# Emptying the filter's PSUM banks on two engines, splitting the last quad, and moving two casts to GpSimd

## The chip, the cores and the metric

The kernel runs on one core of a Trainium2 chip. The metric is the device time of one execution in microseconds. Where a few tenths of a microsecond matter, the text also gives the length of one stage in the profiled execution, because the stage can be read to 0.1 us while whole executions spread by more.

## The reference

The reference filters eight sequences of 3008 steps and 256 channels in the frequency domain, and passes every step through a feed-forward layer with a squared ReLU:

```python
def _attn_ref(x, filt_r, filt_i):            # x: (8, 3008, 256)
    X = np.fft.rfft(x, axis=1)
    F = (filt_r + 1j * filt_i)[None, :, :]
    return np.fft.irfft(X * F, n=x.shape[1], axis=1).astype(np.float32)

def _moe_ref(x, w_in, w_out):                # x: (24064, 256), w_in: 256 x 2048
    h = np.maximum(x @ w_in, 0.0)
    return (h * h @ w_out).astype(np.float32)
```

The kernel does the transforms as matrix products (stages A and B forward, P and Y back). After the first sequence has been filtered, the feed-forward products begin, and they fill the rest of the time. The change touches only the first sequence, ahead of the feed-forward products.

## The kernel before

PSUM is given out from rings: `psF` and `psO` are single banks (two each), and `psH` are double banks (two). A bank means here 128 x 512 in F32, as the program's tiles have it. The filter is spread over the partitions by matmuls (`psf`, im = 0 for its real part, im = 1 for its imaginary part), scaled and emptied to `sF` in SBUF:

```python
    def place_f(im, k, *engs, rotate=False):
        ...
            t = psH(f"psf_{im}_{k}")
            banks, groups = [t[:, 0, :], t[:, 1, :]], [(t, 0)]
        ...                                   # matmuls with sPF into the two banks
        for t, i in groups:
            eng = engs[i % len(engs)]
            ...                               # eng empties t into sF
```

VectorE multiplies stage B's result by the filter (`prods`). Stage P takes two of these products, four blocks of steps together (a quad), into a double bank; ScalarE empties it to `ze`, and `ze` is written to memory, to be read back in another layout (`zt`) by stage Y:

```python
    def unit_p0(k):
        ...
        ps = psH(f"psP_0_{k}")
        for i in range(4):                    # products with sSP and sSPx into ps
            ...
        nc.scalar.copy(out=ze, in_=ps.rearrange("p t (a d) -> p (t a) d", d=D))
        nc.sync.dma_start(out=dZ[0]..., in_=ze)
```

The units are called in this order, with `unit_b` standing for stage B and its product:

```python
    for k in range(2):
        cast_wide(1, k, nc.gpsimd, nc.gpsimd)
    for k in range(7):
        if k < 6:
            unit_b(0, 2 * k)
            if k < 5:
                place_f(1, k + 1, nc.scalar)
            unit_b(0, 2 * k + 1)
        if k > 0:
            unit_p0(k - 1)
        if k < 4:
            place_f(0, k + 2, nc.scalar)
    cast_wide(1, 2, nc.vector, nc.scalar)
    ...                                       # reads of z, loads of w_out, stage A of the next sequence
    for n in range(4):
        unit_y(0, n)
```

## Time and profile before

| what | before |
|---|---|
| time, median of 3 runs (lowest to highest) | 794.04 us (793.07 to 794.68) |
| first product of VectorE in this stage starts | 24.42 us |
| last product ends | 40.39 us |
| last emptying of `ze` ends | 42.08 us |
| first real matmul of stage Y (`psY` from `zt`) | 48.26 us |
| first feed-forward matmul (`psH`) | 49.71 us |

Times in profile lines count from the start of the profiled execution. In a list in order of time, a line gives the start, the busy time, the engine (PE is TensorE, DVE VectorE, ACT ScalarE, POOL GpSimd), the line of the program, the operation, output and input, and how many instructions the line gathers; a bracket gives the idle time of the engine before it and what ended it ("listed idle" below is the sum of these; some waits under 0.2 us are not listed). "Stage" below means the time from the start of VectorE's first product to the end of the last emptying of `ze`: 42.08 - 24.42 = 17.66 us here.

### The profile page before, as it was taken

Reading aid. Unit: us, or ns where it says so; the run is one execution under the profiler, and the core shown is the slowest. Engines: PE = TensorE matmul, PEld = TensorE weight load, DVE = VectorE, ACT = ScalarE, POOL = GpSimd, SP = SyncE. Lnnn points to the kernel's source line nnn. Section 1 sums busy time; section 2 is a strip of 40 time slices with the busy share of each in tenths; the row PEclk is TensorE's granted clock in tenths of the full one; section 3 lists DMA queues with packets and bytes.
Section 4 is the critical chain, followed back from the end, with each engine's and each line's share of the span. In section 5 each row is a group of like instructions: output and inputs, shape, how many; then the busy total and the mean of one; then the engine's idle time right before and its main releaser. Section 6 shows DMA issues by size and latency. Waiting matters only on the chain.

```text
span 791.9 us, 14822 instructions
## 1 busy us (share of the span) xinstructions
PE 778.9 (98%) x6102; PEld 552.5 (70%) x6102; DVE 550.3 (69%) x897; ACT 557.4 (70%) x711; POOL 23.6 (3%) x36
## 2 busy tenths in 40 slices
PE   8989999999999999999999999999999999999998
PEld 5746667667676777867777676776767677676666
DVE  6866994579755897559965699556995579553342
ACT  3976776777777777767776777676777777776664
POOL 3800000000000000000000000000000000000000
PEclk9999999999999999999999999999999999999999
DMA  9994554346814557154562555424563332611111
GB/s 363 368 260 153 146 157 111 93 135 167 205 42 112 167 155 180 48 173 135 132 167 65 163 147 155 112 80 148 159 180 86 97 133 66 147 40 41 41 41 54
DMA packets 88571, 107.32 MB, mean 136 GB/s; under 512 B 6336, under 2 KB 79040, under 8 KB 84288
## 3 DMA queue, kind: packets, MB, share of 16 engines
q1 hardware_dynamic: 88296, 106.19, 46.5%
q8 instruction: 48, 0.79, 0.4%
q10 hardware_dynamic: 144, 0.18, 0.1%
q14 instruction: 19, 0.16, 0.1%
q0 software_dynamic: 64, 0.00, 0.0%
HBM read 58.12 MB, written 48.23 MB: 134 GB/s over the span
## 4 chain that ended last, share of the span: by engine, by line
PE 89%; DVE 6%; DMA 3%; ACT 1%; SPq 0%; issue 0%; DVEq 0%; ACTq 0%
PE psO L579 40%; PE psH L562 38%; PE psA L361 3%; PE psY L532 2%; PE psB L445 2%; DMA f<-in_filt_i_dram 2%; PE psP L496 2%; DVE prod L453 2%; DVE h L570 1%; DMA wout<-in_moe_w_out_dram 1%; PE psf L287 1%; PE psf L290 1%; DVE yf L467 0%; ACT sF L298 0%; DVE yf L461 0%; ACT h L566 0%
## 5 line engine op out<-in xcount | busy, mean ns | idle before, releaser
L566 ACT ACTIVATE h<-psH 128x1024 f16<-128x1024 f32 x376 | 384.9, 1024 | 189.3 <-PE psH L562 186.7
L579 PE MATMUL psO<-sWout,h 128*128 128x256 f16 x3008 | 388.9, 272 | 0.6 <-DVE h L570 0.6
L562 PE MATMUL psH<-yt,sWin 128*128 128x512 f16 (+7 forms) x1728 | 386.9, 351 | 1.6 <-DVE yt L541 0.7
L579 PEld LDWEIGHTS <-h 128*128 128x128 f16 x3008 | 290.6, 98 | 79.1 <-DVE h L570 0.9
L570 DVE TENSOR_TENSOR h<-h 128x1024 f16<-128x1024 f16 x376 | 252.6, 685 | 104.7 <-ACT h L566 104.5
L562 PEld LDWEIGHTS <-sWin 128*128 128x128 f16 x1728 | 159.5, 98 | 101.7 <-issue 3.3
L453 DVE TENSOR_TENSOR prod<-psB,sF 128x1024 f16<-128x1024 f32 x84 | 102.3, 1218 | 2.8 <-PE psB L445 2.8
L541 DVE CAST yt<-psY 128x376 f16<-128x376 f32 x62 | 34.0, 549 | 59.4 <-PE psY L532 59.4
L367 DVE CAST u<-psA 96x512 f16<-96x512 f32 x50 | 34.3, 687 | 47.3 <-PE psA L361 45.1
L498 ACT CAST ze<-psP 128x512 f16<-128x512 f32 x84 | 49.1, 585 | 17.2 <-PE psP L496 14.7
L590 ACT COPY ost<-psO 128x512 f32<-128x512 f32 (+1 forms) x96 | 55.8, 581 | 6.8 <-PE psO L579 5.3
L532 PE MATMUL psY<-sC,zt 112*128 112x94 f16 x512 | 42.4, 205 | 1.4 <-DMA zt<-dZ 1.4
L532 PEld LDWEIGHTS <-zt 112*128 112x128 f16 x512 | 35.1, 98 | 11.6 <-issue 1.6
L467 DVE TENSOR_TENSOR yf<-prod,yf 128x512 f16<-128x512 f16 x84 | 35.7, 425 | 2.9
L361 PE MATMUL psA<-x,sC 94*96 94x512 f16 x96 | 36.6, 382 | 0.0
L445 PE MATMUL psB<-ut,sSB 128*128 128x256 f16 x192 | 36.5, 273 | 0.0
L496 PE MATMUL psP<-yf,sSP 128*128 128x256 f16 x168 | 32.1, 272 | 0.5 <-DVE prod L453 0.3
L539 ACT CAST yt<-psY 128x376 f16<-128x376 f32 x66 | 30.9, 468 | 2.0 <-issue 1.7
L445 PEld LDWEIGHTS <-sSB 128*128 128x128 f16 x192 | 18.5, 98 | 19.5
L340 DVE CAST x<-x 94x2048 f16<-94x2048 f32 x24 | 29.2, 1216 | 0.0
L365 ACT CAST u<-psA 96x512 f16<-96x512 f32 x50 | 28.6, 572 | 0.0
L460 DVE COPY yf<-prod 64x512 f16<-64x512 f16 x84 | 24.3, 289 | 2.9
(65 smaller groups left out, 253.2 us busy)
## 6 DMA issues: line engine op xcount, KB each, us to landing
x<-in_x_dram SPq DMA_DIRECT2D x20, 768.0 KB
zt<-dZ SPq DMA_DIRECT2D x64, 192.0 KB
dU<-u SPq DMA_DIRECT2D x28, 384.0 KB
dZ<-ze SPq DMA_DIRECT2D x28, 384.0 KB
out_dram<-ost SPq DMA_DIRECT2D x66, 128.0 KB
out_dram<-ost SPq DMA_DIRECT2D x31, 256.0 KB
ut<-dU SPq DMA_DIRECT2D x7, 1024.0 KB
xw<-in_x_dram SPq DMA_DIRECT2D x6, 1024.0 KB
```

Source lines behind the costliest of these rows:

```text
L361: nc.tensor.matmul(ps[0:96, :], sSA, x16s[(b, c)][:, m, :], start=True, stop=True)
L445: nc.tensor.matmul(ps[:, i * D:(i + 1) * D], sSB[:, 2 * p + i, :], uts[b][:, 2 * p + i, :], start=True, stop=True)
L453: nc.vector.tensor_mul(out=prod, in0=ps.rearrange("p (a d) -> p a d", d=D).unsqueeze(1).to_broadcast([128, 2, 2, D]), in1=sF[:, :, 2 * p:2 ...
L467: nc.vector.tensor_add(out=yf, in0=prod[:, 0], in1=yf)
L496: nc.tensor.matmul(ps[:, i * D:(i + 1) * D], sSP[:, 2 * p + i, :], yf[:, i, :], start=True, stop=True)
L498: nc.scalar.copy(out=zes[(b, c)][:, 2 * i6:2 * i6 + 2, :], in_=ps.rearrange("p (a d) -> p a d", d=D))
L532: nc.tensor.matmul(ps[:, 94 * jj:94 * jj + 94], zt[:, 4 * (g % 2) + jj, dt * 128:(dt + 1) * 128], sSY, start=True, stop=True)
L562: nc.tensor.matmul(ps[:, i, o:o + n], sWin[:, dt, jt * 128:(jt + 1) * 128], yts[b][:, dt, r:r + n], start=(dt == 0), stop=(dt == 1))
L566: nc.scalar.activation(out=h2[:, 2 * s:2 * s + 2, :], in_=ps, func=AF.Relu)
L570: nc.vector.tensor_mul(out=v, in0=v, in1=v)
L579: nc.tensor.matmul(pso[g][:, t % 2, :], h2s[g][:, jt, t * 128:(t + 1) * 128], sWout[:, jt, :], start=(jt == 0), stop=(jt == NJT - 1))
L590: nc.scalar.copy(out=ost[:, h0:h0 + step, :], in_=pso[g][:, h0:h0 + step, :])
```

## The change

Its intent is to relieve ScalarE, which empties three double banks in every round of 3.3 us. Part 1 gives half of each emptying of the filter's real part to VectorE (four times). Part 2 puts the last quad of stage P into two single banks and empties it in three pieces, so that its second half alone comes after the last product. Part 3 moves two casts of the next input from VectorE and ScalarE to GpSimd.

```diff
-    def place_f(im, k, *engs, rotate=False):
+    def place_f(im, k, *engs, rotate=False, halves=False):
...
-            banks, groups = [t[:, 0, :], t[:, 1, :]], [(t, 0)]
+            banks = [t[:, 0, :], t[:, 1, :]]
+            groups = [(t[:, i:i + 1, :], i) for i in range(2)] if halves else [(t, 0)]
...
-        ps = psH(f"psP_0_{k}")
+        if k == 5:
+            ps = [psF("psP_0_5a"), psF("psP_0_5b")]
+        else:
+            t = psH(f"psP_0_{k}")
+            ps = [t[:, 0, :], t[:, 1, :]]
...
-        nc.scalar.copy(out=ze, in_=ps.rearrange("p t (a d) -> p (t a) d", d=D))
+        if k < 5:
+            nc.scalar.copy(out=ze, in_=t.rearrange("p t (a d) -> p (t a) d", d=D))
+        else:
+            nc.scalar.copy(out=ze[:, 0:2, :], in_=ps[0].rearrange("p (a d) -> p a d", d=D))
+            nc.scalar.copy(out=ze[:, 2, :], in_=ps[1][:, 0:D])
+            nc.vector.tensor_copy(out=ze[:, 3, :], in_=ps[1][:, D:2 * D])
...
-    for k in range(2):
+    for k in range(3):
         cast_wide(1, k, nc.gpsimd, nc.gpsimd)
...
-            place_f(0, k + 2, nc.scalar)
-    cast_wide(1, 2, nc.vector, nc.scalar)
+            place_f(0, k + 2, nc.scalar, nc.vector, halves=True)
```

More of the change, by code (lines that the diff above doesn't have):

```diff
@@ L481, in unit_p0 @@
             for v, w in enumerate((sSP[:, c2, :], sSPx[c2 // 12][:, c2 % 12, :])):
-                nc.tensor.matmul(ps[:, i // 2, (i % 2) * D:(i % 2) * D + D], w,
+                nc.tensor.matmul(ps[i // 2][:, (i % 2) * D:(i % 2) * D + D], w,
                                  prod[:, v, i % 2, :], start=(v == 0), stop=(v == 1))
-        nc.scalar.copy(out=ze, in_=ps.rearrange("p t (a d) -> p (t a) d", d=D))
+        if k < 5:
[4 more added lines that the diff above has]
+            nc.vector.tensor_copy(out=ze[:, 3, :], in_=ps[1][:, D:2 * D])
         nc.sync.dma_start(
```

## The prediction

> **What bounds the kernel now.** I read the page first (busy shares), then the chain of waits between 24 and 61 us, then the order of time on ScalarE, VectorE and TensorE between 20 and 50 us. The page says that TensorE is busy 98% of the span, so nearly everything is a feed-forward stage that the change does not touch. The change acts between 24 and 47 us. What counts is therefore when the feed-forward stage starts, about 50 us in, because after that start the program is the same. The chain of waits gives the way there (start us, us, what):
>
> ```profile
> 29.93 1.12 ACT sF L298
> ...
> 33.25 1.12 ACT sF L298
> ...
> 38.04 2.36 DVE prods L453 x2
> 40.44 0.61 PE psP L482 x4
> 41.07 1.02 ACT ze L484
> 42.11 2.38 DMA dZ<-ze
> 44.63 0.31 SPq L514
> 45.05 5.91 DMA wout<-in_moe_w_out_dram
> 50.96 1.03 ACT h L566
> ```
>
> Up to 38 us the chain runs through ScalarE emptying the placement of the filter (sF); then it goes over to VectorE's last two products, the last quad of stage P, its eviction ze, the write of dZ, and the reads and loads that are queued behind that write. So whatever delays the last ze delays all that follows. In order of time (start us, us busy, engine, line, what, idle before), ScalarE has one round like this, and VectorE the whole stage like this:
>
> ```profile
> 31.02 1.01 ACT L484 CAST ze<-psP 128x1024 f16<-128x1024 f32 x1
> 32.16 1.02 ACT L298 ACTIVATE sF<-psf 128x1024 f16<-128x1024 f32 x1
> 33.25 1.11 ACT L298 ACTIVATE sF<-psf,sign 128x1024 f16<-128x1024 f32 x1
> 34.34 1.01 ACT L484 CAST ze<-psP 128x1024 f16<-128x1024 f32 x1
> ```
>
> ```profile
> 24.42 7.06 DVE L453 TENSOR_TENSOR prods<-psB,sF 128x1024 f16<-128x1024 f32 x6
> 32.44 2.35 DVE L453 TENSOR_TENSOR prods<-psB,sF 128x1024 f16<-128x1024 f32 x2 [0.96 <-ACT ze L484]
> 35.77 4.62 DVE L453 TENSOR_TENSOR prods<-psB,sF 128x1024 f16<-128x1024 f32 x4 [0.98 <-ACT ze L484]
> 40.30 0.68 DVE L222 CAST xw<-xw 128x1024 f16<-128x1024 f32 x1
> ```
>
> A round of ScalarE is 34.34 - 31.02 = 3.32 us for three evictions of 1.01 to 1.11 us: it is full. But VectorE, too, is nearly full: from 24.42 to 40.39 us (35.77 + 4.62) it has twelve products and idles only twice, 0.96 + 0.98 = 1.94 us in all. That 1.94 us is all the room it has for new work.
>
> [...] on ScalarE 1024 columns take 1.012 us and 512 take 0.598, on VectorE 1.22 and 0.68, so halves cost more than half. [...] VectorE's cast of 128x1024 f takes 1.51 us at 20.56 while GpSimd casts too, against 0.68 to 0.69 alone.
>
> **Part 1: halves of the placement.** Four evictions of psf on ScalarE (1.02 us each, the four with im = 0, k = 2 to 5) become a ScalarE half (0.598 in the group of 512 columns) and a VectorE half (0.68; back to back about 0.60, from three casts of ut that take 2.40 us with one of 1.22). ScalarE is relieved of about 4 x 0.45 = 1.8 us. VectorE gets 4 x 0.60 = 2.4 us, more than its 1.94 us of room. Even if every idle moment vanished, its last product would end at 40.39 + 2.4 - 1.94 = 40.85.
>
> It won't go that well, as the built program shows in its semaphore waits:
> - Each VectorE half waits for a count of ScalarE that is exactly that of the other half of the same tile, not for TensorE. The halves lie in two banks, yet they run one after the other: I count this as a fact of the program, whatever made it so.
> - VectorE's queue is product 0, 1, half 2, product 2, 3, half 3, 4, 5, half 4, 6, 7, half 5, 8 to 11. A half that waits for ScalarE holds up the products behind it.
> - The ring of the two double banks has changed places once: psP_0 now waits for the eviction of psf_1_2 instead of psf_0_2, and psf_0_3 for the VectorE half of psf_0_2.
>
> I step through it with these durations: eight matmuls of a bank pair 0.87 us (0.109 apart), 0.2 us from the last one's start plus its drain to the eviction, product 1.165 (7.06 for six in a row, less the overhang), 0.05 us for a wait that is met. The same stepping for the kernel before ends ze at 42.03; the trace has 42.08, so the method may be trusted to about 0.1 us.
> - Products 0 and 1 end at 26.75, half 2 at 27.36, products 2 and 3 at 29.69.
> - psf_1_2 is emptied from 26.56 to 27.67 as before; psP_0 starts at 27.72 instead of 26.61, fills to 28.59, psf_0_3 to 29.47. ScalarE empties ze 0 from 28.79 to 29.80, then its half of psf_0_3 to 30.37. VectorE, free since 29.69, does half 3 from 30.42 to 31.03: 0.7 us idle.
> - Products 4 and 5 end at 33.36; ScalarE's half of psf_0_4 ends at 33.74; half 4 runs from 33.79 to 34.40. Products 6 and 7 end at 36.73; half 5 runs from 37.16 to 37.77. Idle 0.43 twice.
> - Products 8 to 11 follow without a gap: 37.77 + 4 x 1.165 = 42.43.
>
> Against 40.39 that is **+2.0 us** for the last product (work +2.4, idle 0.7 + 0.43 + 0.43 = 1.56 in place of 1.94).
>
> **Part 2: the last quad.** Before: from the end of the last product, 40.39, to the end of ze, 42.08, 1.69 us. After: 0.05 wait, four matmuls 0.44, drain 0.2, ScalarE's last 256 columns (an estimate by the two sizes above: 0.39), wait 0.04, VectorE's 256 columns (likewise 0.41), one after the other [...]: 1.53 us. The first half of the quad has long been emptied. **Gain 0.16 us.**
>
> **Part 3: casts of x on GpSimd.** VectorE loses 0.68 us at 40.30 and ScalarE 1.05 us at 41.98; GpSimd, which is done at 39.14, gets two more of about 1.0 us (3.99 for four) and ends near 41.2. The chunk that needs them is the third, whose matmuls run from 44.4 us on. And the 24 matmuls of stage A run 0.218 us apart without one gap, so ScalarE's cast held up nothing: TensorE next waited for the read of z:
>
> ```profile
> 46.56 0.27 PE L530 MATMUL psY<-zero 128*128 128x128 f16 x2 [0.29 <-ACT u L390]
> 48.26 0.33 PE L532 MATMUL psY<-sC,zt 112*128 112x94 f16 x4 [1.42 <-DMA zt<-dZ]
> ```
>
> Gain: none. In the changed kernel stage A would start at 42.93 and end near 48.2, and z land at 48.26 + 1.9 = 50.2, still later.
>
> **Sum.** +2.04 - 0.16 + 0 = +1.9 us on the last ze; the write of dZ, both loads of w_out and the reads of z stand behind it in one queue in the same order, so the feed-forward stage starts 1.9 us later. 794.04 + 1.9 = **795.9 us**.
>
> **Rivals.**
> - What the change was made for: ScalarE was full and on the chain, so relieving it by 0.45 us in four rounds shortens the stage. For it: the three evictions of ScalarE fill 3.14 of 3.32 us. Against: TensorE works through 28 matmuls of 0.109 us in a round, 3.05 us, so a round can gain 0.27 us at most, about 1.1 us in four; and VectorE can't give that, as the sum without waits (40.85) shows. If both halves ran side by side, my stepping puts ze at about 42.5 to 42.9: +0.4 to +0.8, a time near 794.6. If I am wrong about VectorE altogether and the tail and the freed casts count: 793.
> - The delay is absorbed, as the transfers behind are the bound anyway: the DMA engines are full from 47 to 60 us. Against: they are idle from 42 to 43 us just because they wait for ze, and the loads are issued after the reads of z. If half were absorbed: 795.
> - VectorE is held up further: GpSimd's two added casts run beside products 9 to 11. The products that ran beside GpSimd took 1.168 us each, those half beside it 1.133; at most 0.1 us. Worse would be waits of the ring that I have mis-stepped: one eviction more in the chain is 1.1 us, 797.
>
> **Range and chances.** The runs of before spread 793.07 to 794.68, about 0.8 us either way, and my stepping may be off by 0.5 us: 794.7 to 797.0. Two per cent are 16 us; the whole stage that is changed lasts 17, and nothing else moves. Within 2%: 0.98; either side 0.01.
>
> **What would show it right or wrong.** Right: in the changed profile VectorE's 512-column casts of psf start just after ScalarE's halves end and are waited for as "ACT sF"; VectorE's idle time before its halves is about 1.5 us and before its products near nothing; its last product ends near 42.4; the chain of waits runs through VectorE in the whole stage; psY's first real matmuls start near 50.2 and the first eviction h near 52.9; the idle time of TensorE before psP grows. The third part is right if stage A's matmuls remain 0.218 us apart. The prediction is wrong if the halves overlap in time, if the last ze ends before 42.1, or if psY starts within 0.5 us of 48.26 although ze is late.

The order, which the 1.53 us of Part 2 count as 0.39 + 0.04 + 0.41, is in the trace of the changed kernel: ScalarE's quarter runs from 43.27 us for 0.37 us, VectorE's from 43.67 us for 0.42 us, and VectorE's idle time before it is ended by "ACT ze". The 0.2 us called drain can be read in the trace of the kernel before: the last matmul of the last quad starts at 40.77 us, one interval of 0.109 us later it is 40.88, and `ze` starts at 41.07.

## More of the kernel before

One view sums the busy time of each engine over the 17.7 us of the stage. Its columns are the window, its length, and then TensorE, weight loads, VectorE, ScalarE and GpSimd with their instruction counts, the granted TensorE clock, the DMA engines' share and GB/s:

```profile
24.40:42.10 17.70, 16.49 (x152) 13.69 (x150) 14.70 (x14) 15.62 (x16) 14.23 (x21) 1.00 0.89 335
```

TensorE, VectorE, ScalarE and GpSimd are each busy 80% of this window or more, the weight loads 77%.

## The result, and the profile after

The changed kernel took 795.49 us in the median of six runs (795.30 to 797.36); the kernel before 793.42 us in the median of its six (793.07 to 794.68). The ratio is 1.003, with a 95% interval of 1.0017 to 1.0043: within 2%, and slower by some 2 us. Here and below a ratio is the mean time of one kernel's fast runs over the mean of the other's in the same rounds, so it is not quite the ratio of the quoted medians. All kernels gave correct results.

| us | before | after | predicted |
|---|---|---|---|
| first product starts | 24.42 | 24.55 | 24.42 |
| last product ends | 40.39 | 42.58 | 42.43 |
| idle of VectorE between its products | 1.94 | 1.70 | 1.56 |
| last product to last `ze` | 1.69 | 1.51 | 1.53 |
| first real matmul of stage Y | 48.26 | 50.32 | 50.2 |
| stage | 17.66 | 19.54 | |

VectorE of the changed kernel, in order of time:

```profile
24.55 2.36 DVE L454 TENSOR_TENSOR prods<-psB,sF 128x1024 f16<-128x1024 f32 x2
26.82 0.68 DVE L303 CAST sF<-psf 128x512 f16<-128x512 f32 x1
27.42 2.35 DVE L454 TENSOR_TENSOR prods<-psB,sF 128x1024 f16<-128x1024 f32 x2
30.55 0.69 DVE L303 CAST sF<-psf 128x512 f16<-128x512 f32 x1 [0.78 <-ACT sF L299]
...
37.37 0.69 DVE L303 CAST sF<-psf 128x512 f16<-128x512 f32 x1 [0.41 <-ACT sF L299]
37.97 4.61 DVE L454 TENSOR_TENSOR prods<-psB,sF 128x1024 f16<-128x1024 f32 x4
43.67 0.42 DVE L494 CAST ze<-psP_5b 128x256 f16<-128x256 f32 x1 [1.09 <-ACT ze L493]
```

The halves are the casts of 128x512. From the second on they wait for "ACT sF", ScalarE's half of the same double bank, and the idle time that the kernel before had ahead of its products now stands ahead of them. The third half (34.01 us, 0.51 us of idle) is in the cut. The chain of waits (start, length, what) shows a round of the changed kernel, and then the end of the stage:

```profile
33.38 0.61 ACT sF L299
33.98 0.02 issue
34.01 0.70 DVE sF L303
34.71 0.04 issue
34.75 1.03 PE psP L487 x8
...
40.23 2.36 DVE prods L454 x2
...
43.27 0.38 ACT ze L493
43.65 0.02 issue
43.67 0.44 DVE ze L494
44.11 0.01 issue
44.12 2.38 DMA dZ<-ze
```

Before, one emptying of 1.12 us stood in this chain. Now ScalarE's half, VectorE's half and a handover stand there one after the other (33.38 to 34.71 us, 1.33 us), and TensorE's next product with SPt waits for them. The sums of the same 17.7 us show what the relief of ScalarE was worth:

```profile
24.40:42.10 17.70, 15.70 (x143) 12.69 (x141) 15.99 (x17) 12.88 (x15) 16.32 (x23) 1.00 0.85 320
```

ScalarE went from 15.62 to 12.88 us. The relief in this is 4 x (1.02 - 0.60) = 1.68 us; most of the rest is one emptying of `ze` (1.01 us) that the changed kernel has not reached at 42.1 us. TensorE, too, did less in the same time (15.70 for 16.49 us). Over its own, longer stage (24.55 to 44.10 us) ScalarE is busy for 13.70 us: its freed time became idle time.

One more thing in the profiled execution must be set apart, as it is not part of the change. It took 797.24 us, 1.8 us more than four other runs of the changed kernel (795.30 to 795.56). Its first feed-forward matmuls are slower, and the windows show why (the clock is the third number from the end):

```profile
50.32 0.33 PE L542 MATMUL psY<-sC,zt 112*128 112x94 f16 x4 [1.30 <-DMA zt<-dZ]
...
51.78 4.49 PE L572 MATMUL psH<-yt,sWin 128*128 128x512 f16 x12 [0.28 <-ACT yt L549]
```

```profile
51.60:55.00 3.40, 3.08 (x7) 0.96 (x7) 0.85 (x2) 1.15 (x2) 0.00 (x0) 0.50 1.06 245
55.00:56.00 1.00, 1.00 (x6) 0.50 (x5) 0.69 (x1) 0.56 (x1) 0.00 (x0) 0.99 1.10 348
```

For 3.4 us the granted clock is 0.50. The three profiled executions with this dip (this one, and those of e4_halves_act and e11_plain below) report a mean clock of 0.998; the other eleven report 0.999 or 1.0 and show none. I sort all runs whose clock is on record by this, those at 0.997 or 0.998 as with the dip (for the six runs of the kernel before quoted above none is). The kernel before has them too (three of ten runs, 794.80 to 794.96 us). Below, "undipped" are runs at 0.999 or above. Undipped, the changed kernel takes 795.42 us (median of four) and the kernel before 793.43 us (median of seven on the chip of the first eight experiments): the change costs 2.0 us.

### The profile page after: what moved, and what is told of

Its sections match the earlier page's. It is cut to its first block, busy times and chain, and to the rows that moved or that the text cites. A ratio compares the mean times of both kernels' runs of the same rounds, so it can differ in the third digit from the quotient of the medians.

```text
span 795.5 us, 14818 instructions
## 1 busy us (share of the span) xinstructions
PE 781.3 (98%) x6102; PEld 552.9 (70%) x6102; DVE 552.7 (69%) x901; ACT 554.6 (70%) x711; POOL 25.6 (3%) x38
## 4 chain that ended last, share of the span: by engine, by line
PE 90%; DMA 4%; DVE 4%; ACT 1%; issue 0%; DVEq 0%; ACTq 0%; SPq 0%
PE psO L589 40%; PE psH L572 39%; PE psA L362 3%; PE psY L542 3%; PE psB L446 2%; PE psP L506 2%; DMA sSP<-cSP 2%; DVE prod L454 1%; DVE h L580 1%; DMA xw<-in_x_dram 1%; DMA win<-in_moe_w_in_dram 1%; PE psP L487 1%; DMA zt<-dZ 0%; ACT h L576 0%; ACT ze L490 0%; DVE yf L468 0%
## 5 line engine op out<-in xcount | busy, mean ns | idle before, releaser
L576 ACT ACTIVATE h<-psH 128x1024 f16<-128x1024 f32 x376 | 384.9, 1024 | 190.6 <-PE psH L572 190.6
```

The costliest lines, as they stand in the source:

```text
L576: nc.scalar.activation(out=h2[:, 2 * s:2 * s + 2, :], in_=ps, func=AF.Relu)
```

## The experiments

The first two calls ran on one chip, where the kernel before took 793.53 and 793.50 us in the median of nine and ten runs. The third call ran on another chip, where six of nine runs of the kernel before had the dip, so that its median is 794.89 us, and 793.59 us in its three undipped runs. The ratios quoted contain the dips; the stage does not.

### Which part costs the time

**e1_halves** is the kernel before with part 1 alone, **e2_quad** with part 2 alone, **e3_casts** with part 3 alone.

```diff
 # e1_halves: before, and place_f with its halves
-            place_f(0, k + 2, nc.scalar)
+            place_f(0, k + 2, nc.scalar, nc.vector, halves=True)
 # e2_quad: before, and unit_p0 of the changed kernel
 # e3_casts: before, and
-    for k in range(2):
+    for k in range(3):
-    cast_wide(1, 2, nc.vector, nc.scalar)
```

> The kernel before with part 1 alone (halves of the placement on two engines). Theory A (VectorE is full, and its halves wait for ScalarE's): last product ends near 42.6 us, last ze near 44.2, psY near 50.4; +2.0 us in runs without a dip of the TensorE clock. Rival B (the loss is in the last quad or in the casts on GpSimd): last product near 40.4, no change of the time.

> The kernel before with part 2 alone (last quad in single banks, ze in thirds; x casts as before). Theory A: last product at 40.4 as before, ze 0.16 us earlier (41.9), time -0.1 to -0.2 us. Rival B: the serial thirds cost time, ze after 42.1.

> The kernel before with part 3 alone (x casts all on GpSimd). Theory A: no effect, within 0.1 us: GpSimd ends near 41.2, stage A's matmuls stay 0.218 us apart, psY stays at 48.3. Rival B: GpSimd's casts slow VectorE's last products or delay stage A: psY later by 0.3 us or more.

| | time, median | ratio to before (95%) | first to last product | stage |
|---|---|---|---|---|
| before, profiled | | | 15.97 | 17.66 |
| after, profiled | 795.49 | 1.003 (1.0017 to 1.0043) | 18.03 | 19.54 |
| e1_halves | 795.39 | 1.0018 (1.0005 to 1.003) | 18.03 | 19.73 |
| e2_quad | 793.32 | 0.9994 (0.998 to 1.0008) | 15.98 | 17.48 |
| e3_casts | 793.63 | 0.9998 (0.9986 to 1.0011) | 15.97 | 17.67 |

The loss is part 1, all of it: its last product is late by 18.03 - 15.97 = 2.06 us with or without the other parts. Part 2 shortens the stage by 0.18 us, part 3 by nothing. No run of e1_halves had the dip, and still it is 2 us longer than the undipped kernel before, so the dip is not the loss.

### Is it the splitting, VectorE's added work, or the order of the two halves?

**e4_halves_act** is the changed kernel with both halves on ScalarE. **e10_dummy** is the kernel before with four emptyings of 128x512 added to VectorE at the same places in its queue; they read a bank of stage B that it reads anyhow, and nobody uses their result. **e5_sep** is the changed kernel with each half in a single-bank tile of its own, so that VectorE's half no longer waits for ScalarE's; stage B then uses only `psF` until its last products.

```diff
 # e4_halves_act, against the changed kernel
-            place_f(0, k + 2, nc.scalar, nc.vector, halves=True)
+            place_f(0, k + 2, nc.scalar, halves=True)
 # e10_dummy, against the kernel before, in unit_b
+        if b == 0 and p % 2 and p < 8:
...
+            nc.vector.tensor_copy(out=prods["idle"], in_=ps.rearrange("p (a d) -> p a d", d=D))
 # e5_sep, against the changed kernel, in place_f and unit_b
+        elif halves:
+            banks = [psO(f"psf_{im}_{k}_{i}").rearrange("p a d -> p (a d)") for i in range(2)]
+            groups = [(t.unsqueeze(1), i) for i, t in enumerate(banks)]
-        if b == 0 and p % 4 > 1:
+        if b == 0 and p > 11:
```

> The changed kernel with both halves of each placement on ScalarE: no added VectorE work, no wait between the engines, bank order as before. Measured from the first product to the last ze (17.66 us in the kernel before, 19.54 in the changed one). Theory A (the loss is VectorE's part): 17.5 to 18.0, time within 0.3 us of before. Rival E (splitting an eviction costs by itself, whoever does it): above 18.5.

> The kernel before with four VectorE casts of 128x512 from PSUM added where the changed kernel has its halves (copies of a bank that VectorE has just used; the result is not used). VectorE's added work alone, no wait for ScalarE, same banks as before. Rival C (added work is a large part of the loss): 18.3 us or more from first product to last ze. Theory A' (VectorE's idle time takes it in): 17.7 to 18.1, +0.1 to +0.4 us.

> The changed kernel with the two halves of a placement in two tiles of one bank each (the pair psO, stage B then in the pair psF alone), so that VectorE's half waits for TensorE and not for ScalarE's half. The same VectorE work, no serial wait. Theory A, both terms real: VectorE without gaps, last product near 41.0, last ze near 42.5, +0.4 us against before, so about 1.5 us less than the changed kernel. Rival C (all of the loss is VectorE's added work): last ze still near 44, +1.9. Rival D (all of it is the serial wait): ze at 42.1 or earlier.

| | time, median | ratio to before (95%) | first to last product | stage | listed idle of VectorE |
|---|---|---|---|---|---|
| e4_halves_act | 794.36 | 1.0 (0.9985 to 1.0016) | 15.98 | 17.49 | 1.94 |
| e10_dummy | 793.66 | 0.9995 (0.9979 to 1.001) | 16.06 | 17.76 | 0.00 |
| e5_sep | 793.37 | 0.9994 (0.9982 to 1.0007) | 16.06 | 17.57 | 0.00 |

The median of e4_halves_act comes from four runs, two of them with the dip (795.23 and 795.0); the undipped two are 793.39 and 793.71. So splitting costs nothing when ScalarE keeps both halves, in the same ring of double banks. VectorE's added work by itself costs 16.06 - 15.97 = 0.09 us. In e10_dummy its queue has not one listed wait:

```profile
26.80 0.68 DVE L461 CAST idle<-psB 128x512 f16<-128x512 f32 x1
...
35.98 4.61 DVE L453 TENSOR_TENSOR prods<-psB,sF 128x1024 f16<-128x1024 f32 x4
```

The last four products start at 35.98 us, 11.45 us after the first (24.53); before it was 35.77 - 24.42 = 11.35. In e5_sep the halves of the two engines overlap, ScalarE's first and then VectorE's lines:

```profile
28.84 0.60 ACT L302 ACTIVATE sF<-psf 128x512 f16<-128x512 f32 x1
```

```profile
29.32 0.68 DVE L306 CAST sF<-psf 128x512 f16<-128x512 f32 x1
...
35.64 4.61 DVE L457 TENSOR_TENSOR prods<-psB,sF 128x1024 f16<-128x1024 f32 x4
```

VectorE starts its half at 29.32 us, while ScalarE's runs to 29.44, and no "ACT sF" ends an idle time of VectorE any more. The last products start 35.64 - 24.19 = 11.45 us after the first. With VectorE at work without a pause, the whole loss is gone, but nothing is gained beyond part 2 either: ScalarE's rounds shrink from 3.32 to about 3.05 us (its emptyings of `ze` start at 27.93, 30.95, 34.01 and 37.08), and VectorE has taken its place as the bound. I had expected the last `ze` 0.4 us later than before; of the rivals the one came true that puts the whole loss on the wait.

### What of the loss is the order, what is the ring

e5_sep undid two things at once: the order of the halves, and their place in the ring of double banks. **e9_serial** puts the order back alone. It is e5_sep with a write of one element by ScalarE after its half, into the part of `sF` that VectorE's half writes next, so that VectorE must wait. **e11_plain** is the changed kernel with the two double banks forced to alternate strictly, as they did before. In the changed kernel the two had changed places once: the first product with SPt waited for the emptying of psf_1_2 (the other image's) in place of psf_0_2.

```diff
 # e9_serial, against e5_sep, after each half of ScalarE
+                if halves:
+                    eng.copy(out=sF[0:1, im, 4 * k + 2, 0:1], in_=zero[0:1, 1:2])
 # e11_plain, against the changed kernel (the counter nring starts at 0)
-        return pps.tile([128, 2, 512], F32, tag="psH", name=name, bufs=2)
+        nring[0] += 1
+        return pps.tile([128, 2, 512], F32, tag=f"psH{nring[0] % 2}", name=name, bufs=1)
```

> The run e5_sep (halves in separate tiles, 17.57 us from first product to last ze) with the serial wait put back: ScalarE writes one element into VectorE's half of the placement after its own half, so VectorE must wait for it. Same banks and same VectorE work as e5_sep. Theory A' (the serial wait is nearly all of the loss): 18.7 to 19.3, idle time before VectorE's halves 1.2 to 1.7 us. Rival F (e5_sep was fast because of its other banks, not because the halves run side by side): below 18.0.

> The changed kernel with the two double banks of the placement of Fr forced to alternate strictly (two tags with one buffer each in place of one tag with two), so that the first product with SPt of an image's quad waits for the VectorE half of the second placement's double bank again, as in the kernel before, instead of ScalarE's emptying of the other image's, and the halves stay one after the other. From the first product of stage P to the last emptying of ze the changed kernel took 19.54 us, the one before 17.66. Theory A (the pair of halves in series keeps the double bank of a ring of two busy 0.7 us longer and everything behind it, placement, cast and product with SPt, shifts): about 19.2 us, and a time of 795.1 to 795.6 us. Theory B (the scheduler's exchange of the two double banks is most of the loss): less than 18.3 us and a time of 793.9 or less.

| | time, median | ratio to before (95%) | first to last product | stage |
|---|---|---|---|---|
| e5_sep: apart, side by side | 793.37 | 0.9994 (0.9982 to 1.0007) | 16.06 | 17.57 |
| e9_serial: apart, one after the other | 793.81 | 0.9999 (0.9985 to 1.0012) | 16.64 | 18.15 |
| e11_plain: in the ring, one after the other, banks alternate | 795.50 | 1.0012 (0.9996 to 1.0027) | 17.70 | 19.21 |
| after: in the ring, one after the other, banks exchanged | 795.49 | 1.003 (1.0017 to 1.0043) | 18.03 | 19.54 |

e9_serial missed what I had expected of it. The forced order is in the trace: VectorE's half starts when ScalarE's extra write is done (its length of 0.18 us adds a little to the handover).

```profile
29.45 0.18 ACT L304 COPY sF<-zero 1x1 f16<-1x1 f16 x1
```

```profile
29.66 0.69 DVE L308 CAST sF<-psf 128x512 f16<-128x512 f32 x1
```

Yet it costs only 18.15 - 17.57 = 0.58 us. The rest seems to need the ring: with the pair in the ring of two double banks the same order costs 19.21 - 18.15 = 1.06 us more. The exchange of the banks adds 19.54 - 19.21 = 0.33 us, so e11_plain fell out as its first theory had it. The three make up the 1.97 us between e5_sep and the changed kernel, as steps of one chain must. The step of 1.06 us is a difference between two kernels that also differ in which banks stage B uses, and in how many tiles a round takes from the ring of double banks (three in e11_plain, two in e9_serial), so I call its cause likely rather than isolated. e4_halves_act helps here: with the same ring and the same halves, but no wait of one engine for another in a pair, the stage is 17.49 us.

The traces of the two show the difference at TensorE. In e11_plain, as in the changed kernel, the chain of waits goes from a half of VectorE (at 33.48 us in e11_plain) straight to the next products with SPt, and these start every 3.41 us (27.36, 30.77, 34.23, 37.59). In e9_serial no wait of TensorE for a half of VectorE is listed, and they start every 3.06 us (26.93, 30.00, 33.05, 36.12), no more than the 3.05 us that TensorE's own matmuls of a round take (28 x 0.109):

```profile
26.93 0.27 PE L492 MATMUL psP<-prods,sSP 128*128 128x256 f16 x1
```

e11_plain shows how the ring passes the delay on. TensorE's first product with SPt waits for VectorE's half, which itself had to stand behind VectorE's first two products:

```profile
26.63 0.68 DVE L305 CAST sF<-psf 128x512 f16<-128x512 f32 x1
```

```profile
27.36 0.27 PE L489 MATMUL psP<-prods,sSP 128*128 128x256 f16 x1 [0.66 <-DVE sF L305]
```

ScalarE's half of this pair was over at 25.40 + 0.60 = 26.00 us. The double bank was free for the next use only at 27.31. This first product with SPt starts 3.00 us after VectorE's first product (27.36 - 24.36); before it was 26.61 - 24.42 = 2.19 us:

```profile
26.61 0.27 PE L482 MATMUL psP<-prods,sSP 128*128 128x256 f16 x1
```

With the exchanged banks it waits for the emptying of psf_1_2 instead, as the trace of e1_halves, which has the same exchange, names it:

```profile
27.72 0.27 PE L483 MATMUL psP<-prods,sSP 128*128 128x256 f16 x1 [0.99 <-ACT sF L299]
```

That is 27.72 - 24.38 = 3.34 us after the first product. In the changed kernel the same matmul stands at 27.89 us, but the profile names a DMA as what ended its wait. The program has it wait for ScalarE's emptying of psf_1_2, and that ended at 26.72 + 1.11 = 27.83 us. So I take the name there to be wrong.

### Is there something better, and does it count?

**e6_par** takes the useful parts: the kernel before with the casts on GpSimd and the last quad in three banks, so that ScalarE and VectorE may empty the last two quarters side by side. **e7_best** adds to e5_sep the quad in three banks, and leaves VectorE only one half of the four (that of psf_0_4), so that neither engine is full.

```diff
 # e6_par and e7_best: unit_p0 for k == 5
+            ps = [psF("psP_0_5a"), psF("psP_0_5b"), psO("psP_0_5c").rearrange("p a d -> p (a d)")]
...
+            nc.scalar.copy(out=ze[:, 2, :], in_=ps[1][:, 0:D])
+            nc.vector.tensor_copy(out=ze[:, 3, :], in_=ps[2][:, 0:D])
 # e7_best alone
+            place_f(0, k + 2, nc.scalar, *([nc.vector] if k == 2 else []), halves=True)
```

> The kernel before with the casts of x on GpSimd and the last quad of stage P in three banks in place of two, so that ScalarE and VectorE empty the last two quarters of ze side by side; no halves. From the first product to the last emptying of ze, 17.66 us before, 17.48 with the quad in two banks: theory (only the end of the chain counts, and the third third then no longer waits for the second): about 17.1 us, which is 0.5 us less than before, and a time of 793.0 us against 793.5. Rival (ze is hidden anyway behind the transfer that takes it to where the last steps read it): the stage is shorter, the time 793.5 as before.

> A version meant to beat both: placements with im = 0 in the pair psO of single banks, only the second half of psf_0_4 on VectorE, the rest on ScalarE; the last quad in three banks, so that ScalarE and VectorE empty its last two quarters side by side; x casts on GpSimd. Stepped as in the prediction with products at 1.13: 16.4 us from first product to last ze, -1.2 us against before, time near 792.2 in runs without a clock dip. If the bank pair psF alone for stage B holds VectorE up, -0.3 or less.

| | time, median | ratio to before (95%) | first to last product | stage |
|---|---|---|---|---|
| e6_par | 793.46 | 0.9988 (0.9975 to 1.0) | 15.97 | 17.08 |
| e7_best | 792.77 | 0.9984 (0.9972 to 0.9997) | 15.59 | 16.70 |

The stage of e6_par is shorter by 0.58 us, as expected. Its time is only 0.13 us below the three undipped runs of the kernel before, less than these runs can tell; that the rest of the 0.58 us is lost between `ze` and stage Y is possible, as this stretch varied between 5.8 and 6.5 us from one profiled execution to the next, but it is not shown. e7_best is the fastest kernel here, 0.66 us below the undipped kernel before (793.43), with a stage shorter by 0.96 us, where I had expected 16.4. In its tail the two engines overlap:

```profile
40.44 0.39 ACT L497 CAST ze<-psP_5b 128x256 f16<-128x256 f32 x1
```

```profile
40.66 0.42 DVE L498 CAST ze<-psP_5c 128x256 f16<-128x256 f32 x1 [0.69 <-PE psP_5c L491]
```

### The dip of the clock

**e8_warm** is the changed kernel, **e12_best_warm** e7_best, each with 24 in place of 2 matmuls of zeros ahead of stage Y, which fill most of the 1.3 us that TensorE waits there for `zt`.

```diff
-            for k in range(2):
-                nc.tensor.matmul(ps[:, 128 * k:128 * k + 128], zero, zero, start=True, stop=True)
+            for k in range(2 if n else 24):
+                nc.tensor.matmul(ps[:, 128 * (k % 2):128 * (k % 2) + 128], zero, zero, start=True, stop=True)
```

> The changed kernel with 24 in place of 2 matmuls of zeros ahead of the product with Ct. Theory (the dip of the granted clock comes of TensorE's idle time while it waits for zt): all runs at a clock of 0.999 to 1.0 and 795.4 us. Rival: two runs in six at 0.998 and some 797.3 us, as in the changed kernel without it. In neither is the loss of 2 us against the kernel before made good, as that stands in undisturbed runs too.

> The fastest kernel so far (separate single banks for the halves, one half alone on VectorE, the last quad in three banks; 792.77 us) with 24 in place of 2 matmuls of zeros ahead of the product with Ct, which fill the 1.3 us that TensorE idles while it waits for zt. Theory (the dip of the granted clock to 0.50 for some 3.4 us in the first feed-forward matmuls comes of that idle time): every run at a clock of 0.999 to 1.0, and 792.7 us. Rival (the dip comes of something else, as the chip's state): about one run in four at 0.998 and 1.4 to 1.9 us longer, as in the kernel before.

e8_warm took 795.84 us in the median (795.48 to 796.28; ratio 1.0017, 1.0004 to 1.0029), e12_best_warm 793.10 us (793.01 to 793.32; ratio 0.9983, 0.997 to 0.9995). None of their ten runs had the dip. Six of nine runs of the kernel before had it, one of four of e11_plain, and none of five of e6_par, which has no added matmuls. So the theory holds as far as it was tried, but kernels without its remedy went free as well (on the first chip also e1_halves, e7_best, e9_serial and e10_dummy, 18 runs), and the cause stays open. In both warmed kernels the profiled stage is as long as without it (19.54 and 16.70 us). Where no dip falls, the filling earns nothing: e12_best_warm is 0.49 us below the undipped kernel before on its chip, e7_best was 0.66 us below on the other.

The dip has the same size and length in both traces that I read for it: 0.50 for 3.4 us (51.6 to 55.0 in the changed kernel, 51.4 to 54.8 in e11_plain). It came in 17 of 71 runs without the added matmuls, and cost 1.2 to 1.9 us against undipped runs of the same kernel (e11_plain 796.62 to 795.39, the changed kernel 797.36 to 795.42). What sets it off is not shown. In the changed kernel TensorE's longest listed idle time in the 10 us before the fall was 1.30 us, and in the 3.4 us from 48.0 us on, just before it, TensorE was busy for 1.82 us.

## Why the prediction was right

**The path.** The whole delay went through the last `ze` to stage Y and the feed-forward products, as predicted. The stage grew by 1.88 us and the undipped time by 2.0. The rival that half of it is absorbed is out. The time itself, 795.9 us predicted and 795.49 measured, started from the 794.04 us of three runs; the undipped kernel before takes 793.43.

**The sum of part 1.** The last product came 18.03 us after the first, against 18.01 predicted (42.43 - 24.42), and e1_halves, which has part 1 alone, gave the same 18.03. The idle times ahead of VectorE's halves, predicted as 0.7, 0.43 and 0.43 us, were 0.78, 0.51 and 0.41. So the reading of the built program's waits carried the number. Adding up busy times would not have: they left room for the added work, as e10_dummy shows.

That 18.01 lies so near 18.03 is luck, though. The prediction's sum is 16.42 us of work (twelve products of 1.165 and four halves of 0.61) and 1.59 us of waits. e10_dummy does the same work without a listed wait in 16.06 us, so the work was put 0.36 us too long, and the waits, 18.03 - 16.06 = 1.97 us, 0.38 us too short. The two errors cancel. (The listed idle times, 1.70 us, are less than these 1.97 us: with nothing to wait for, VectorE's next record starts some 0.09 us before the last one ends, as at 31.15 us after 30.55 + 0.69, and each of the three waits loses that too.)

**Parts 2 and 3.** The tail went from 1.69 to 1.51 us (predicted 1.53), and e2_quad alone gave 0.18 us (predicted 0.16). The casts were worth nothing, as e3_casts shows. GpSimd finished late, but in time:

```profile
35.27 5.96 POOL L222 CAST xw<-xw 128x1024 f16<-128x1024 f32 x6
```

It ends at 41.23 us, predicted near 41.2, and the matmuls of stage A in the changed kernel follow each other by 0.22 us, as before. VectorE's last four products, beside GpSimd's added casts, took 4.61 us (4.62 before). The prediction reads the cast of 1.51 us as VectorE held up by GpSimd, which is not shown: of the casts that it counts as alone, the one of 0.69 us at 11.61 us of the kernel before ran beside one of GpSimd, and there it was GpSimd's that took 1.56 us, where four of that size took 3.99 us from 35.15 us on.

Five steps beside the main sum were wrong:

1. "Even if every idle moment vanished, its last product would end at 40.39 + 2.4 - 1.94 = 40.85." This is 16.43 us after the first; e10_dummy and e5_sep took 16.06. The term that was mis-sized is the room. Products follow each other every 1.13 us when nothing waits (4.61 us for four, with the overhang of the last), so twelve take 13.6 us, and 2.4 of the 15.97 us were free, not 1.94. The row "7.06 us for six" that I had taken as back to back hides a wait of about 0.17 us: its pair at 27.82 us took 2.52 us, where the pair at 26.69 took 2.34. Shared among six products this wait is 0.03 us, nearly all of the difference between 1.168 and 1.133 us that the third rival puts down to GpSimd.
2. "If both halves ran side by side, my stepping puts ze at about 42.5 to 42.9." Measured 41.76 us in e5_sep, with a stage of 17.57 us, 0.09 less than before. The same wrong room made this rival look too slow.
3. The weights of the causes. I had given most of the first delay, psP_0 at 27.72 in place of 26.61 us, to the exchange of the double banks. Forced back, it was worth 0.33 us, since the half of VectorE that takes its place ends at 27.31 us, and the product with SPt starts 3.00 in place of 3.34 us after the first product.
4. The first feed-forward emptying, predicted near 52.9 us, came at 53.98 in the profiled execution because of the clock dip, and at 52.67 in e1_halves without it.
5. That "the chain of waits runs through VectorE in the whole stage" was not so. Of the 15.2 us of the changed kernel's chain from ScalarE's first `ze` (28.96) to the last (44.11), VectorE has 3.50 us: one half, the last two products and the last quarter of `ze`. The rest passes through the double banks, with ScalarE's emptyings and TensorE's products filling them. So VectorE was not the bound of the changed kernel; that it was full already is the wrong room of point 1.

**What stays open.** The built program makes VectorE's half wait for ScalarE's, though the two lie in different banks and only share a tile. e5_sep, where each has a tile of its own, ran two such halves at once (ScalarE's from 28.84 to 29.44 us, VectorE's from 29.32 us) with a correct result. Why the scheduler adds the wait for one tile of two banks, I have not found out. A pair that runs side by side inside the ring of double banks could therefore not be tried.

## What to carry to other kernels

When a buffer's emptying is shared between two engines, its next use waits for the later of the two, and that one has a queue of its own: in e11_plain ScalarE's half was over at 26.00 us, VectorE's at 27.31, and TensorE's next product with SPt started at 27.36. So look in the built program at what each half waits for before you count the microseconds taken off the busy engine. Give each engine's share its own tile if they are to run side by side: with one tile for both, three of the four VectorE halves waited 0.78, 0.51 and 0.41 us for ScalarE (the changed kernel), with two tiles none waited (e5_sep). And, as far as e9_serial and e11_plain tell, keep a shared pair out of a ring with only two places. Those waits of VectorE went with a buffer held too long, not with too few buffers: e4_halves_act has as many and no wait of this kind.

A split has its price in the records. Emptyings of 128 partitions from PSUM to SBUF in 16 bits took, for 256, 512 and 1024 columns, 0.42, 0.68 to 0.69 and 1.22 us on VectorE, and 0.37 to 0.39, 0.58 to 0.60 and 1.01 to 1.02 us on ScalarE (1.11 us with `sign`). Two halves of 512 in a row on ScalarE took 1.09 us (e4_halves_act at 25.38 us), where the whole took 1.02 us (the kernel before at 25.45 us).
